# Weight granules of an attention and two-MLP kernel: one sum of squares and one pair of scale operations for two granules instead of one

## The chip, the cores and the metric

The kernel runs on one core of a Trainium2 chip. The metric is the device time of one execution in microseconds (us). Five engines work side by side, each through its own list of instructions in order: TensorE (PE in the profile, PEld for its weight loads), VectorE (DVE), ScalarE (ACT), GpSimd (POOL) and SyncE (SP), which here issues the transfers.

## The reference

```python
scores = scale * np.matmul(q, k.transpose(0, 1, 3, 2))      # 4 batches, 8 heads, 576 positions, 64 per head
masks = [mask_local if h < H // 2 else mask_strided ...]     # a window of 32, or every 32nd position
attn = softmax(np.where(masks, scores, -1e9))
x = np.matmul(attn, v)                                       # -> 2304 tokens of 512
h = x @ w_in                                                 # 512 -> 2048
g = (a0 + a1*h + a2*h*h + a3*h*h*h) / (1 + |b0|*|h| + |b1|*h*h + 1e-6)
x = g @ w_out                                                # 2048 -> 512
h = x @ w_in2                                                # 512 -> 1024
solu = h * softmax(h)
out = (layer_norm(solu) * g_ln) @ w_out2                     # 1024 -> 512
```

The weights arrive as 64-bit floats. All products of the two MLPs have float32 accuracy, made from 16-bit operands.

## The kernel before, in words

A product with float32 accuracy is made of three 16-bit matmuls: high part times high part, high times low, low times high. So each weight has two 16-bit tiles, for `w_in` `wi_h` and `wi_l`, for `w_out` `wo_h` and `wo_l`, and before the split each block of a weight is multiplied by a power of two that brings it into the range of a 16-bit float.

The two large weights come in eight granules each. A granule of `w_in` ("wi") is 256 of its 2048 columns, which is what one group of the first product needs; a granule of `w_out` ("wo") is 64 of its 512 output columns. So a block of 128 output columns of the second product needs two wo granules, and all four blocks need all eight. For each granule:

- SP loads the 64-bit words (`w_load`) into a staging place; most of these are tiles that are free at that time, such as `wo_h`, `ysb` or `ws`.
- `w_conv` makes 32-bit floats of them with three bit operations on DVE (L151, L152, L153) into a tile `T`, into a piece of `gtb` or `ysb`, or into a place of staging that is done with.
- ACT squares them and sums along each partition (L160). The sum goes to `ss`, a small tile of which there are two. PE adds it over the partitions with a matrix of ones (L84). DVE makes from the exponent of the sum the power of two `pat` (L163) and its inverse `scl` (L164).
- `w_split` writes the high part on ACT (L181), and on DVE the low part (L182), which needs the high part.

The first batch of the attention (12 units: scores on PE, maximum and sums on DVE, exponentials on ACT, a product on POOL, transposes and the product with v on PE) runs from the start to about 66 us, while `w_in` is loaded and converted. After it the first product starts. It is made of groups of 256 columns of `h` and blocks of 256 tokens, 72 groups: 24 matmuls in `mm_h` (L532 to L534) into `ps_h`, of which there are two, then the rational function on ACT, POOL and DVE (ACT L540 to L571, POOL L549 and L553, DVE L557 to L583), which gives `ps_h` free again at L583, then the high and low parts of the result (ACT L593, POOL L597), then 24 matmuls of the second product in `mm_y` (L609 to L611). The later batches of the attention, the conversion of the second MLP's weights and the second MLP itself are interleaved with these groups.

The order of the instructions on every engine isn't written out by hand. A scheduler plays the program through with a model of its own and places instructions by when they would be ready and by a priority that `prio` sets; each engine then runs its list in that order. An instruction that waits therefore holds up everything behind it on its engine.

The lines of the code around the change, in the main part: wi granules are converted and split one after the other with priorities 10000 + 300 g, wo granules in `wo_work` with `p_step(g)`, two in each of the first four steps:

```python
    for g in range(8):
        prio(10000 + 300 * g)
        w_conv("wi", g)
        w_split("wi", g)
```

Of the kernel before, what the change touches and what calls it, by code (L numbers as in the profile page):

```python
# [8 lines left out]
F32 = mybir.dt.float32  # L9
# [3 lines left out]
AF = mybir.ActivationFunctionType  # L13
# [27 lines left out]
def kernel(ctx: ExitStack, tc: tile.TileContext, qk, v, w_in, w_out, ab, w_in2, w_out2, gln, out):  # L41
    nc = tc.nc
    PE, ACT, DVE, POOL, SP = nc.tensor, nc.scalar, nc.vector, nc.gpsimd, nc.sync

    const = ctx.enter_context(tc.tile_pool(name="const", bufs=1))
# [15 lines left out]
    gtb = wts.tile([128, NGT, 2, 2, TB], F16, name="gtb")  # L61
    ysb = wts.tile([128, NYS, 2, KD, TB], F16, name="ysb")
# [10 lines left out]
    def psum(tag, shape=(128, 512), bufs=1):  # L73
        return ps.tile(list(shape), F32, tag=tag, name=f"ps_{tag}", bufs=bufs)

    def t1(name, n=1, bufs=2):
        return tiny.tile([128, n], F32, tag=name, name=name, bufs=bufs)

    def ew(name, bufs, shape=(128, 512), dt=F32):
        return big.tile(list(shape), dt, tag=name, name=name, bufs=bufs)  # L80

    def sum_over_partitions(x):
        t = psum("a", bufs=2)[:, 0:x.shape[1]]
        PE.matmul(t, lhsT=ones_f, rhs=x, start=True, stop=True)  # L84
        return t
# [9 lines left out]
    NGRAN = {"wi": 8, "wo": 8}  # L95
    pat = {k: const.tile([128, n], F32, name=f"pat_{k}") for k, n in NGRAN.items()}
    scl = {k: const.tile([128, n], F32, name=f"scl_{k}") for k, n in NGRAN.items()}
# [21 lines left out]
    def w_load(name, g):  # L119
        if name == "wi":  # L120
            src = w_in.bitcast(I32)[:, g * 512:(g + 1) * 512].rearrange("(k p) f -> p k f", p=128)
        elif name == "wo":
            src = w_out.bitcast(I32)[:, g * 128:(g + 1) * 128].rearrange("(k p) f -> p k f", p=128)
        elif name == "wi2":
            src = w_in2.bitcast(I32)[g * 128:(g + 1) * 128, :]
        else:
            src = w_out2.bitcast(I32)[g * 256:(g + 1) * 256, :].rearrange("(k p) f -> p k f", p=128)
        t = w_slot(name, g)
        if name == "wi2":
            SP.dma_start(out=t, in_=src)  # L130
        else:
            SP.dma_start(out=t.rearrange("p (k f) -> p k f", f=src.shape[2]), in_=src)
        stg[name, g] = t

    def w_conv(name, g):
        t = stg.pop((name, g))
        if name in ss2:
            if g == 2:
                w2t[name] = ew("ws", 1, (128, 2048), I32).bitcast(F32)
            T = ew("T", 2, (128, 1024), F32) if g < 2 else w2t[name][:, 1024 * (g - 2):1024 * (g - 1)]  # L140
        elif name == "wo" and g % 5 > 1:
            T = ysb[:, 2].rearrange("p h d t -> p (h d t)") if g == 4 else gtb[:, 2 * (g % 5) - 4:2 * (g % 5) - 2].rearrange("p b c h t -> p (b c h t)")
            T = T.bitcast(F32)
        else:
            T = spare.pop() if spare else ew("T", 2, (128, 1024), F32)
        if name == "wi" and g < 7:
            spare.append(t[:, 0:1024].bitcast(F32))
        t = t.rearrange("p (f two) -> p f two", two=2)
        lo, hi = t[:, :, 0], t[:, :, 1]
        Ti = T.bitcast(I32)  # L150
        DVE.tensor_scalar(Ti, hi, 3, 0x3FFFFFFF, op0=ALU.logical_shift_left, op1=ALU.bitwise_and)  # L151
        DVE.scalar_tensor_tensor(Ti, lo, 29, Ti, op0=ALU.logical_shift_right, op1=ALU.bitwise_or)  # L152
        DVE.scalar_tensor_tensor(Ti, hi, -0x40000000, Ti, op0=ALU.bitwise_and, op1=ALU.bitwise_or)  # L153
        tt[name, g] = T
        if name in ss2:
            ACT.activation(ew("ot", 1).bitcast(F16), T, AF.Square, accum_out=ss2[name][:, g:g + 1])
            return
        ss = t1("ss")
        src, junk, _ = w_parts(name, g, T)
        ACT.activation(junk, src, AF.Square, accum_out=ss)  # L160
        sg = sum_over_partitions(ss)
        p, s = pat[name][:, g:g + 1], scl[name][:, g:g + 1]
        DVE.tensor_scalar(p.bitcast(I32), sg.bitcast(I32), 1, EXPM, op0=ALU.logical_shift_right, op1=ALU.bitwise_and)  # L163
        DVE.tensor_scalar(s.bitcast(I32), p.bitcast(I32), -1.0, float(EXPM - (51 << 23)), op0=ALU.mult, op1=ALU.add)  # L164

# [3 lines left out]
    def w_parts(name, g, T):  # L169
        if name == "wi":  # L170
            sl = slice(g * 256, g * 256 + 256)
            return T.rearrange("p (k f) -> p k f", k=KD), wi_h[:, :, sl], wi_l[:, :, sl]
        sl = slice(g * 64, g * 64 + 64)
        return T.rearrange("p (k f) -> p k f", k=KF), wo_h[:, :, sl], wo_l[:, :, sl]

    def w_split(name, g):
        s = scl[name][:, g:g + 1]
        if g == NGRAN[name] - 1:
            DVE.tensor_scalar(inv[name], pat[name], 2.0 ** 50, None, op0=ALU.mult)
        src, h_, l_ = w_parts(name, g, tt.pop((name, g)))  # L180
        ACT.activation(h_, src, AF.Copy, scale=s)  # L181
        DVE.scalar_tensor_tensor(l_, src, s, h_, op0=ALU.mult, op1=ALU.subtract)  # L182
# [30 lines left out]
    def w_pmax(name):  # L213
        m = t1("pm")
        DVE.tensor_reduce(m, pat[name], axis=AX.X, op=ALU.max)
        DVE.tensor_scalar(pmax[name], m, 2.0 ** 65, None, op0=ALU.mult)
# [514 lines left out]
    def prio(p):  # L731
        tc.cur_priority = p
# [8 lines left out]
    def p_step(n):  # L741
        return P0 + int(n * P_STEP)
# [53 lines left out]
    for g in range(8):  # L796
        prio(10000 + 300 * g)
        w_conv("wi", g)
        w_split("wi", g)
    prio(900)  # L800
    w_pmax("wi")
    g_scale(0)
# [114 lines left out]
    def wo_work(g):  # L917
        w_conv("wo", g)
        if g + 4 < 8:
            w_load("wo", g + 4)  # L920
        w_split("wo", g)
        if g == 7:
            w_pmax("wo")
            for j in range(2):
                sl = slice(64 * j, 64 * j + 64)
                POOL.tensor_copy(cwo[sl, :], inv["wo"][sl, j::2])

    def w2_work(n):
        for name, n0 in (("wi2", 14), ("wo2", 21)):
            m = n - n0  # L930
            if m == 0:
                w_load(name, 0)
                w_load(name, 1)
            if m in (1, 2):
                for g in (2 * m - 2, 2 * m - 1):
                    w_conv(name, g)
                    if g < 2:
                        w_load(name, g + 2)
                if m == 2:
                    w2_scale(name)  # L940
            if m in (3, 4):
                w2_split(name, 2 * m - 6)
                w2_split(name, 2 * m - 5)

    for n in range(M2S + 4 * (NT2 + 2)):
        if 0 <= n < 4:
            for g in (2 * n, 2 * n + 1):
                prio(p_step(g))
                wo_work(g)
        prio(p_step(n + 2))  # L950
        w2_work(n)
        prio(p_step(n))
        if n >= M2S and (n - M2S) % 8 == 0 and (n - M2S) // 8 < NB:
            y_scale2((n - M2S) // 8)
        step(n)
# [56 lines left out]
```

## Time and profile before

| | |
|---|---|
| time, three runs | 804.7, 797.74, 805.2 us (median 804.7) |
| the profiled execution's own time | 799.58 us |
| its span, first to last instruction | 797.2 us |
| busy share of the span | PE 89%, DVE 72%, ACT 61%, POOL 41% |
| mean granted TensorE clock | 0.928 of full speed |
| chain of work that ended last, by engine | PE 58%, DVE 15%, DMA 5%, ACT 5%, issue 4%, POOL 3% |

A busy share is a mean over stages that have different limits, so the stages are read apart: the windows view gives each engine's busy time in a stretch with the granted clock, the timeline lists one engine's instructions with their start, duration and the idle time ahead of them with what ended it.

### The profile page before, as it was taken

The page shows a single profiled execution, that of the slowest core. Times are in us where ns is not written, and L with a number is a line of the kernel's source. Part 1 is how long each engine was busy: PE and PEld are TensorE (multiplying, and loading weights), DVE is VectorE, ACT ScalarE, POOL GpSimd, SP SyncE. Part 2 cuts the span into 40 slices and gives each one's busy share as a digit, 9 for nine tenths or more (in the row PEclk, how much of TensorE's full clock was granted, in tenths as well). Part 3 has the DMA queues.
Part 4 walks back from the last instruction along what each step waited for, and adds up shares of the span by engine and source line. Part 5 has one row for each costly group of instructions (what it writes and reads, how often), then busy time and mean ns, then how long its engine had stood idle before and what let it go on. Part 6 is the DMA issues. An engine that isn't in the chain of part 4 may idle for free.

```text
span 797.2 us, 14480 instructions
## 1 busy us (share of the span) xinstructions
PE 707.4 (89%) x5422; PEld 539.7 (68%) x5422; DVE 573.0 (72%) x1210; ACT 483.4 (61%) x1143; POOL 327.2 (41%) x312
## 2 busy tenths in 40 slices
PE   4785146988886999899999999999999999999997
PEld 4664135877674788587878777777777777766443
DVE  5788899779869886688987666757657666644562
ACT  3656475756756687866777666646546556543442
POOL 2530303545557567745545443344343434330000
PEclk8565656999999999899999999999999999999999
DMA  9985511053130431113031101011012020111134
GB/s 271 350 207 139 159 53 33 1 171 92 54 118 1 138 86 40 33 28 92 2 72 33 41 1 41 1 41 40 1 41 35 7 40 8 34 41 40 39 80 106
DMA packets 68101, 55.98 MB, mean 70 GB/s; under 512 B 39616, under 2 KB 56000, under 8 KB 67520
## 3 DMA queue, kind: packets, MB, share of 16 engines
q1 hardware_dynamic: 68032, 55.07, 25.8%
q8 instruction: 42, 0.69, 0.4%
q14 instruction: 27, 0.22, 0.1%
HBM read 40.90 MB, written 4.72 MB: 57 GB/s over the span
## 4 chain that ended last, share of the span: by engine, by line
PE 58%; DVE 15%; DMA 5%; ACT 5%; issue 4%; POOL 3%; SPq 0%; DVEq 0%; ACTq 0%; POOLq 0%
PE ps_h L532 6%; PE ps_h L534 6%; PE ps_h L533 6%; PE ps_y L611 6%; PE ps_y L610 6%; PE ps_y L609 6%; PE ps_h L642 3%; PE ps_h L643 3%; PE ps_h L644 3%; PE ps_a L722 3%; PE ps_a L721 3%; PE ps_a L720 3%; PE ps_a L289 2%; DMA wi_h<-in_w_in_dram 1%; PE ps_a L380 1%
## 5 line engine op out<-in xcount | busy, mean ns | idle before, releaser
L532 PE MATMUL ps_h<-xs,wi_h 128*128 128x256 f16 x576 | 160.4, 279 | 12.1 <-DVE p L583 9.2
L533 PE MATMUL ps_h<-xs,wi_h 128*128 128x256 f16 x576 | 160.2, 278 | 0.0
L534 PE MATMUL ps_h<-xs,wi_l 128*128 128x256 f16 x576 | 159.9, 278 | 0.2 <-DVE wi_l L182 0.2
L597 POOL TENSOR_TENSOR gtb<-p,gtb 128x512 f16<-128x512 f32 x56 | 67.1, 1199 | 134.8 <-ACT gtb L593 134.6
L611 PE MATMUL ps_y<-gtb,wo_l 128*128 128x256 f16 x448 | 122.1, 273 | 0.0
L610 PE MATMUL ps_y<-gtb,wo_h 128*128 128x256 f16 x448 | 122.1, 273 | 0.0
L609 PE MATMUL ps_y<-gtb,wo_h 128*128 128x256 f16 x448 | 122.1, 273 | 0.0
L549 POOL TENSOR_SCALAR q<-A,aba 128x512 f32<-128x512 f32 x72 | 62.6, 869 | 108.6 <-ACT A L540 108.5
L553 POOL TENSOR_TENSOR q<-q,A 128x512 f32<-128x512 f32 x72 | 96.6, 1342 | 5.7
L557 DVE TENSOR_TENSOR p<-p,ps_h 128x512 f32<-128x512 f32 x72 | 49.2, 683 | 57.6 <-ACT p L543 53.2
L566 ACT ACTIVATE L<-q 128x512 f32<-128x512 f32 x72 | 45.3, 630 | 70.0 <-POOL q L553 69.8
L575 DVE SCALAR_TENSOR_TENSOR q<-q,ps_h 128x512 f32<-128x512 f32 x72 | 49.2, 683 | 36.5 <-ACT ps_h L571 35.4
L533 PEld LDWEIGHTS <-wi_h 128*128 128x128 f16 x576 | 57.6, 100 | 16.6 <-issue 8.4
L532 PEld LDWEIGHTS <-wi_h 128*128 128x128 f16 x576 | 57.7, 100 | 13.3 <-ACT wi_h L181 3.0
L540 ACT ACTIVATE A<-ps_h,ih 128x512 f32<-128x512 f32 x72 | 49.2, 684 | 28.0 <-PE ps_h L534 26.2
L593 ACT ACTIVATE gtb<-p 128x512 f16<-128x512 f32 x56 | 35.3, 631 | 50.6 <-DVE p L583 50.5
L610 PEld LDWEIGHTS <-wo_h 128*128 128x128 f16 x576 | 56.4, 98 | 10.7
L609 PEld LDWEIGHTS <-wo_h 128*128 128x128 f16 x576 | 56.6, 98 | 10.1
L534 PEld LDWEIGHTS <-wi_l 128*128 128x128 f16 x576 | 57.5, 100 | 8.2 <-DVE wi_l L182 0.3
L340 POOL TENSOR_TENSOR e<-e,arc 96x508 f32<-96x508 f32 (+3 forms) x36 | 37.4, 1039 | 62.2 <-DVE arc L339 48.6
L611 PEld LDWEIGHTS <-wo_l 128*128 128x128 f16 x576 | 56.4, 98 | 8.1 <-issue 1.1
L331 ACT ACTIVATE e<-ps_a,amx 96x127 f32<-96x127 f32 (+2 forms) x132 | 45.8, 356 | 16.8 <-DVE amx L315 12.7
(336 smaller groups left out, 1825.0 us busy)
## 6 DMA issues: line engine op xcount, KB each, us to landing
qkb<-in_qk_dram SPq DMA_DIRECT2D x28, 304.0 KB, 4.5
out_dram<-ot SPq DMA_DIRECT2D x18, 256.0 KB, 2.5
wo_l<-in_w_out_dram SPq DMA_DIRECT2D x4, 1024.0 KB, 5.4
wo_h<-in_w_out_dram SPq DMA_DIRECT2D x4, 1024.0 KB, 5.3
vl<-in_v_dram SPq DMA_DIRECT2D x4, 768.0 KB, 5.3
wi_h<-in_w_in_dram SPq DMA_DIRECT2D x3, 1024.0 KB, 7.0
wi_l<-in_w_in_dram SPq DMA_DIRECT2D x3, 1024.0 KB, 5.2
wo_h<-in_w_in_dram SPq DMA_DIRECT2D x3, 1024.0 KB, 16.5
```

The costliest lines, as they stand in the source:

```text
L532: PE.matmul(o, lhsT=wi_h[:, k, f:f + 128], rhs=xs[i][:, 0, k, :], start=(k == 0), stop=False)
L533: PE.matmul(o, lhsT=wi_h[:, k, f:f + 128], rhs=xs[i][:, 1, k, :], start=False, stop=False)
L534: PE.matmul(o, lhsT=wi_l[:, k, f:f + 128], rhs=xs[i][:, 0, k, :], start=False, stop=(k == KD - 1))
L540: ACT.activation(A, t, AF.Abs, scale=gsc[i]["ih"][:, g:g + 1])
L549: POOL.tensor_scalar(w["q"], w["A"], aba[:, 5:6], aba[:, 4:5], op0=ALU.mult, op1=ALU.add)
L553: POOL.tensor_tensor(w["q"], w["q"], w["A"], op=ALU.mult)
L557: DVE.tensor_tensor(w["p"], w["p"], hp[i, g], op=ALU.mult)
L575: DVE.scalar_tensor_tensor(w["q"], w["q"], EPS_D, w["r"], op0=ALU.add, op1=ALU.mult)
L597: POOL.tensor_tensor(t[:, :, 1, :], gw.pop((i, g))["p"].rearrange("p (c t) -> p c t", t=TB), t[:, :, 0, :], op=ALU.subtract)
L609: PE.matmul(o, lhsT=wo_h[:, f, w], rhs=gg[:, c, 0, :], start=(f == 0 and d % 2 == 0), stop=False, skip_group_check=True)
L610: PE.matmul(o, lhsT=wo_h[:, f, w], rhs=gg[:, c, 1, :], start=False, stop=False, skip_group_check=True)
L611: PE.matmul(o, lhsT=wo_l[:, f, w], rhs=gg[:, c, 0, :], start=False, stop=(f == KF - 1), skip_group_check=True)
```

## The change

Pairs of granules take the step from the sum of squares to the scale together. The sums of squares go to a tile of eight columns for each weight, `ssq`, instead of the two small tiles `ss`. A new function `w_scales` adds two columns over the partitions with one L84 and makes two columns of `pat` and `scl` with one L163 and one L164. For wi, all eight conversions stand ahead in the program; the scale steps and splits follow pair by pair. For wo, the scale step and both splits stand after the second conversion of a pair. The tile into which a wo granule is converted is chosen with period 4 instead of 5: granules 2, 3, 6 and 7 go to `gtb`, granules 0, 1, 4 and 5 to `T`; before, 2, 3 and 7 went to `gtb`, 4 to `ysb`, and 0, 1, 5 and 6 to `T`.

```diff
-        elif name == "wo" and g % 5 > 1:
-            T = ysb[:, 2].rearrange("p h d t -> p (h d t)") if g == 4 else gtb[:, 2 * (g % 5) - 4:2 * (g % 5) - 2].rearrange("p b c h t -> p (b c h t)")
-            T = T.bitcast(F32)
+        elif name == "wo" and g % 4 > 1:
+            j = 2 * (g % 4) - 4
+            T = gtb[:, j:j + 2].rearrange("p b c h t -> p (b c h t)").bitcast(F32)
...
-        ss = t1("ss")
         src, junk, _ = w_parts(name, g, T)
-        ACT.activation(junk, src, AF.Square, accum_out=ss)
-        sg = sum_over_partitions(ss)
-        p, s = pat[name][:, g:g + 1], scl[name][:, g:g + 1]
+        ACT.activation(junk, src, AF.Square, accum_out=ssq[name][:, g:g + 1])
+
+    ssq = {k: const.tile([128, n], F32, name=f"ssq_{k}") for k, n in NGRAN.items()}
+
+    def w_scales(name, g0, n):
+        sg = sum_over_partitions(ssq[name][:, g0:g0 + n])
+        p, s = pat[name][:, g0:g0 + n], scl[name][:, g0:g0 + n]
         DVE.tensor_scalar(p.bitcast(I32), sg.bitcast(I32), 1, EXPM, op0=ALU.logical_shift_right, op1=ALU.bitwise_and)
         DVE.tensor_scalar(s.bitcast(I32), p.bitcast(I32), -1.0, float(EXPM - (51 << 23)), op0=ALU.mult, op1=ALU.add)
...
     for g in range(8):
         prio(10000 + 300 * g)
         w_conv("wi", g)
-        w_split("wi", g)
+    for g0 in range(0, 8, 2):
+        prio(10000 + 300 * g0)
+        w_scales("wi", g0, 2)
+        for g in range(g0, g0 + 2):
+            prio(10000 + 300 * g)
+            w_split("wi", g)
...
         w_conv("wo", g)
         if g + 4 < 8:
             w_load("wo", g + 4)
-        w_split("wo", g)
+        if g % 2 == 2 - 1:
+            w_scales("wo", g + 1 - 2, 2)
+            for j in range(g + 1 - 2, g + 1):
+                prio(p_step(j))
+                w_split("wo", j)
```

The scheduler places the instructions of the whole program anew. In the changed kernel the line numbers are higher: L160, L163, L164, L181 and L182 are L159, L166, L167, L184 and L185 there, and lines of the later functions are three higher. The three places below are the ones that matter for what follows.

ACT at the end of the first attention batch. `q<-ps_a`, `xs<-ps_a` and `tail<-ps_a` belong to the last attention units; the L160 rows (L159 in the change) are the squares of wi granules, named by the place that their 32-bit values lie in. Before:

```order
L358 ACTIVATE q<-ps_a 108x2x108
L411 ACTIVATE xs<-ps_a,xsc_184 128x8x6 x2
L408 ACTIVATE tail<-ps_a 128x2x6
L160 ACTIVATE wi_h,ss<-wi_l 128x4x256
L160 ACTIVATE wi_h,ss<-wo_h 128x4x256
L160 ACTIVATE wi_h,ss<-ysb 128x4x256
L181 ACTIVATE wi_h<-T,scl_wi 128x4x256
L160 ACTIVATE wi_h,ss<-wo_h 128x4x256 x2
L181 ACTIVATE wi_h<-wi_h,scl_wi 128x4x256
```

And in the change, from the square of granule 6 on:

```order
L159 ACTIVATE wi_h,ssq_wi<-wo_h 128x4x256
L361 ACTIVATE q<-ps_a 108x2x108
L334 ACTIVATE p,smb_104<-ps_y,amx 108x108 x2
...
L361 ACTIVATE q<-ps_a 108x4x108
L159 ACTIVATE wi_h,ssq_wi<-wo_l 128x4x256
L414 ACTIVATE xs<-ps_a,xsc_186 128x8x12 x2
...
L184 ACTIVATE wi_h<-T,scl_wi 128x4x256
L184 ACTIVATE wi_h<-wi_h,scl_wi 128x4x256
```

Six of the eight squares of wi move from behind the attention units to places among them, and the eight splits follow one another.

DVE where the wo granules are scaled. L557 to L583 (L560 to L586 in the change) belong to the rational function of groups 0 and 1. Before:

```order
L163 TENSOR_SCALAR pat_wo<-ps_a 128x1
L182 SCALAR_TENSOR_TENSOR wo_l<-T,scl_wo,wo_h 128x16x64
L426 TENSOR_SCALAR rg<-pg_743 128x1
L164 TENSOR_SCALAR scl_wo<-pat_wo 128x1
L163 TENSOR_SCALAR pat_wo<-ps_a 128x1
L151 TENSOR_SCALAR T<-ysb 128x1024
...
L182 SCALAR_TENSOR_TENSOR wo_l<-gtb,scl_wo,wo_h 128x16x64
L557 TENSOR_TENSOR p<-p,ps_h 128x512
```

And in the change:

```order
L166 TENSOR_SCALAR pat_wo<-ps_a 128x2
L560 TENSOR_TENSOR p<-p,ps_h 128x512
L167 TENSOR_SCALAR scl_wo<-pat_wo 128x2
L166 TENSOR_SCALAR pat_wo<-ps_a 128x2
L560 TENSOR_TENSOR p<-p,ps_h 128x512
L564 SCALAR_TENSOR_TENSOR p<-p,ac_728,ps_h 128x512
L92 TENSOR_REDUCE vmax_830<-ps_a 128x1
L167 TENSOR_SCALAR scl_wo<-pat_wo 128x2
L564 SCALAR_TENSOR_TENSOR p<-p,ac_728,ps_h 128x512
L185 SCALAR_TENSOR_TENSOR wo_l<-T,scl_wo,wo_h 128x16x64
```

The first steps of groups 0 and 1 now stand ahead of the first wo splits; before, they stood behind four of them. In the whole list four L583 of `ps_h` groups stand ahead of the last wo split, before it was two.

PE at the last sums over the partitions for wo. Before, the last two L84 stand ahead of any matmul of groups 2 and 3:

```order
L350 MATMUL ps_a<-ident,e 127x96 x4
L380 MATMUL ps_a<-pts,vl 64x96 x4
L84 MATMUL ps_a<-ss,ones_f 128x1 x2
```

In the change, groups 2 and 3 and the first six matmuls of the second product stand ahead of the third pair's L84, and the fourth pair's stands here:

```order
L353 MATMUL ps_a<-ident,e 127x96 x4
L383 MATMUL ps_a<-pts,vl 64x96 x4
L612 LDWEIGHTS wo_h
L612 MATMUL ps_y<-wi_h,wo_h 128x256
L613 LDWEIGHTS wo_h
L613 MATMUL ps_y<-wi_h,wo_h 128x256
L84 MATMUL ps_a<-ssq_wo,ones_f 128x2
```

The two matmuls into `ps_y` ahead of it use the third pair's split. On SP, the load of `vs` (the second batch) moves behind the loads of wo granules 6 and 7; before, it stood ahead of both.

## Rows read from the trace of the kernel before

**Rows 1.** The page: busy times of the engines, granted clock in 40 slices.
```profile
PE 707.4 (89%) x5422; PEld 539.7 (68%) x5422; DVE 573.0 (72%) x1210; ACT 483.4 (61%) x1143; POOL 327.2 (41%) x312
...
PEclk8565656999999999899999999999999999999999
```

**Rows 2.** Windows: stretch, its length, busy time (instructions) by engine, clock, DMA share, GB/s.
```profile
66.00:132.00 66.00, 25.20 (x136) 21.61 (x137) 60.62 (x141) 41.51 (x75) 10.89 (x7) 0.55 0.39 106
132.00:260.00 128.00, 110.46 (x993) 93.44 (x991) 103.77 (x220) 84.50 (x221) 73.93 (x68) 0.99 0.23 74
260.00:340.00 80.00, 75.00 (x653) 62.41 (x653) 60.15 (x121) 61.99 (x157) 55.18 (x51) 0.94 0.24 73
340.00:700.00 360.00, 360.00 (x2878) 275.63 (x2878) 252.98 (x520) 225.88 (x494) 159.25 (x149) 1.00 0.14 31
```

**Rows 3.** Timeline of ACT: start, duration (us), line, operation, count, [idle before <-what ended it].
```profile
67.03 1.06 ACT L160 ACTIVATE wi_h<-wi_l 128x1024 f16<-128x1024 f32 x1
...
69.94 1.06 ACT L160 ACTIVATE wi_h<-wo_h 128x1024 f16<-128x1024 f32 x1 [1.76 <-PE ps_a L84]
...
71.00 1.04 ACT L160 ACTIVATE wi_h<-ysb 128x1024 f16<-128x1024 f32 x1
...
80.39 1.04 ACT L160 ACTIVATE wi_h<-wo_l 128x1024 f16<-128x1024 f32 x1
...
85.56 1.15 ACT L181 ACTIVATE wi_h<-wo_l,scl_wi 128x1024 f16<-128x1024 f32 x1 [1.80 <-DVE inv_wi L179]
```

**Rows 4.** Timeline of DVE, 46 to 137 us.
```profile
46.73 0.74 DVE L315 TENSOR_REDUCE amx<-ps_y 126x2 f32<-126x252 f32 x2 [0.41 <-PE ps_y L289]
...
52.07 0.38 DVE L315 TENSOR_REDUCE amx<-ps_h 108x2 f32<-108x216 f32 x1 [0.97 <-PE ps_h L289]
...
77.40 1.28 DVE L182 SCALAR_TENSOR_TENSOR wi_l<-wi_h,scl_wi 128x1024 f16<-128x1024 f32 x1 [2.09 <-ACT wi_h L181]
...
85.33 0.14 DVE L164 TENSOR_SCALAR scl_wi<-pat_wi 128x1 int32<-128x1 int32 x1
85.39 0.16 DVE L179 TENSOR_SCALAR inv_wi<-pat_wi 128x8 f32<-128x8 f32 x1
...
87.30 0.69 DVE L151 TENSOR_SCALAR T<-wo_h 128x1024 int32<-128x1024 int32 x1 [1.69 <-DMA wo_h<-in_w_out_dram]
...
91.09 1.21 DVE L153 SCALAR_TENSOR_TENSOR T<-wo_h,T 128x1024 int32<-128x1024 int32 x1
...
96.37 0.16 DVE L163 TENSOR_SCALAR pat_wo<-ps_a 128x1 int32<-128x1 int32 x1 [0.87 <-PE ps_a L84]
96.45 2.05 DVE L153 SCALAR_TENSOR_TENSOR T<-ysb,T 128x1024 int32<-128x1024 int32 x1
...
104.36 0.69 DVE L151 TENSOR_SCALAR T<-ysb 128x1024 int32<-128x1024 int32 x1 [0.66 <-DMA ysb<-in_w_out_dram]
...
136.23 1.27 DVE L182 SCALAR_TENSOR_TENSOR wo_l<-gtb,scl_wo,wo_h 128x1024 f16<-128x1024 f32 x1
```

**Rows 5.** DMA issues, 62 to 80 us: count, KB each, us to landing.
```profile
wo_l<-in_w_out_dram SPq DMA_DIRECT2D x1, 1024.0 KB, 5.8
vs<-in_v_dram SPq DMA_DIRECT2D x1, 640.0 KB, 4.2
```

**Rows 6.** Timeline of POOL, 88 to 98 us.
```profile
90.04 3.38 POOL L553 TENSOR_TENSOR q<-q,A 128x512 f32<-128x512 f32 x1
...
96.16 1.26 POOL L553 TENSOR_TENSOR q<-q,A 128x512 f32<-128x512 f32 x1
```

**Rows 7.** Timeline of PE: two neighbouring matmuls at the lower clock; the longest later idle time.
```profile
75.12 0.42 PE L533 MATMUL ps_h<-xs,wi_h 128*128 128x256 f16 x1
75.33 0.42 PE L534 MATMUL ps_h<-xs,wi_l 128*128 128x256 f16 x1
...
259.65 0.96 PE L350 MATMUL ps_a<-ident,e 96*127 96x96 f32 x4 [5.05 <-POOL e L340]
```

**Rows 8.** The page: matmuls that start a group, idle time before them and what ended most.
```profile
L532 PE MATMUL ps_h<-xs,wi_h 128*128 128x256 f16 x576 | 160.4, 279 | 12.1 <-DVE p L583 9.2
```

## The prediction

> **What bounds the kernel now.** I read the page first. TensorE is busy for 89% of the span, and its granted clock is low only in the first seven of forty slices, about 140 us [rows 1]. So the question is when TensorE becomes full and what holds it until then. The windows answer it: from 340 to 700 us PE is busy for 360 of 360 us at full clock, and nothing on another engine can shorten that stretch. From 66 to 132 us it is busy for 25.2 of 66 us at a clock of 0.55, while DVE is busy for 60.6 of 66 us. Between 132 and 340 us, PE is idle for 17.5 + 5.0 = 22.5 us [rows 2]. The 66 to 132 us stretch is where the two large weights are converted, scaled and split, so what the change does there is read from DVE's queue: whatever delays the last wo split on DVE (from 136.23 us, [rows 4]) delays the second product, and whatever DVE gets done by then beside the weights is a lead for PE.
>
> Next I looked at why DVE and ACT wait there. The third square of wi starts on ACT only at 67.03 us, and the next one waits for an L84 [rows 3]: there are two `ss` tiles, so a third square has to wait until the first L84 has read its tile, and PE's queue has that L84 behind the last attention unit. The last square of wi runs at 80.39 us and the last high part at 85.56 us. DVE pays for this with 2.09 us at 77.40 us, where it waits for a high part [rows 4].
>
> **The change part by part.** The sum is made against the profiled execution, 799.6 us with a span of 797.2 us. The three runs have a median of 804.7 us, which is 0.6% above it; the mean of all four executions is 801.8 us.
>
> *Squares and splits of wi.* With eight columns of `ssq` no square waits for an L84, and the change's order puts six squares among the attention units, with the eight splits one after another. DVE's 2.09 us go. What is late next is DVE itself: a low part takes it 1.28 us [rows 4], a high part takes ACT 1.15 us [rows 3]. I take 2.1, between 0 and 2.1.
>
> The squares aren't free at their new place. ACT takes its list in order, so each square holds up the attention units behind it until its granule is converted. Start to start a square takes 71.00 - 69.94 = 1.06 us [rows 3], so six cost between nothing and 6.4 us. ACT has room, and DVE gains there: the conversions move up in its list, into four idle times between 46.73 and 52.07 us (0.41, 0.68, 0.37 and 0.97 us, the first and the last in [rows 4]), 2.4 us together. I take 2.4 - 1.0 = 1.4 for both, since the squares stand where ACT waits for PE anyway; the ends are +2.4 and -4.0.
>
> *Fewer scale operations.* Eight L163 and eight L164 go. On DVE such an operation takes 0.14 us but the next starts after 0.06 us (85.33 to 85.39, [rows 4]). So the sixteen are worth 16 x 0.06 = 1.0 us at least and 16 x 0.14 = 2.2 us at most; I take 1.0, because DVE's queue moves on by starts. The eight L84 that go run while PE is idle: nothing.
>
> *Transfers.* DVE waits 1.69 us for the load of wo granule 0 at 87.30 us and 0.66 us for granule 5 at 104.36 us [rows 4]. In the change's list the conversion of granule 0 stands behind the last split of wi instead of ahead of it, and that of granule 5 behind the first four wo splits, so both loads have cover: 2.3, between 0 and 2.3. On the other side `vs` is loaded behind 1 MB more on SP. A load of 1 MB lands after 5.8 us, `vs` after 4.2 us [rows 5], and the maximum over `vs` stands between the third and the fourth wi split, ahead of what gives the staging of granule 0 free. I take -0.5, between 0 and -5.8.
>
> *The pairs of wo.* The first L163 of wo now needs two conversions, two squares and their L84. Before, it waited 0.87 us for one [rows 4]. The second square adds up to 1.06 us; between the conversion and the L163 stand the eight or so small operations of the rational function's constants. I take -0.3, between +0.9 and -1.1.
>
> *PE's queue.* The third pair's L84 is now behind 48 matmuls of groups 2 and 3 and six of the second product. Group 3 may start only when DVE has finished L583 of group 1. Behind this L84 waits DVE's L163, and behind that everything on DVE. At the low clock a group takes 24 x 0.21 = 5.0 us (75.12 to 75.33, [rows 7]). So this costs between nothing, when the squares of granules 4 and 5 are later than group 3, and 5.0 us; I take -3.0, as DVE has L583 of group 1 directly ahead of two conversions of 1.2 us that fill only 2.4 us.
>
> *POOL beside DVE.* Two more groups pass through L549 and L553 while DVE converts. L553 takes 3.38 us at 90.04 us and 1.26 us at 96.16 us; L153 on DVE takes 1.21 us at 91.09 us and 2.05 us at 96.45 us, beside that L553 [rows 4, 6]. Two groups cost DVE between nothing and 2 x 0.84 = 1.7 us; POOL's own 2 x 2.1 us are hidden, since the results are needed later. I take -1.0. The Trainium skill, "SBUF — State Buffer", § Who interferes with whom, says that a DVE instruction with two SBUF inputs and a GpSimd instruction that reads SBUF exclude one another for the whole instruction. The stretched rows agree. By that rule each added L553 could hold DVE for its whole 1.26 us, and this term would be -2.5, the sum 1.5 us smaller.
>
> *What the lead is worth later.* At 259.65 us PE is idle for 5.05 us ahead of four transposes that wait for POOL [rows 7]. In the change's PE list the 24 matmuls of a group stand ahead of these transposes. At full clock they are some 24 x 0.11 = 2.6 us (half of the low clock's 0.21). I take +1.3, between 0 and 2.6.
>
> Sum: 2.1 + 1.4 + 1.0 + 2.3 - 0.5 - 0.3 - 3.0 - 1.0 + 1.3 = 3.3 us saved. Against the profiled execution this is 796.3 us; against the mean of the four executions 798.5 us. As the runs shown lie on both sides I give **798 us**. With all terms at their good ends the change saves 2.1 + 2.4 + 2.2 + 2.3 + 0.9 + 2.6 = 12.5 us (789 us); at their bad ends it saves 1.0 and loses 4.0 + 5.8 + 1.1 + 5.0 + 1.7 = 17.6 us, net 16.6 (818 us), and these need not come together.
>
> **The rivals.** One per cent is 8 us here, about what this kernel's runs can tell from no change.
>
> *The lead removes later waits too (faster).* By the last wo split the change's DVE list holds four L583, before it was two. PE's idle time at the start of a group is 12.1 us, 9.2 of it waiting for L583 [rows 8]. If rational functions stay two groups ahead, these waits go: 3.3 + 9.2 = 12.5 us saved, 789 us. For it speaks that PE's idle time there has this one main cause; against it that the scheduler uses the lead to place the second MLP's conversions differently, so that by group 15 the lists stand alike again.
>
> *PE's queue decides (slower).* The fourth pair's L84 stands behind scores, transposes, the product with v and two matmuls that need the third pair's split, and these wait for ACT, which has the evacuation of the transposes between the two splits. So the two last pairs go one after the other: DVE makes the third pair's scale, ACT splits, PE passes, and only then comes the fourth pair's scale. Each step holds a whole group at the low clock, 5.0 us, and two squares and splits, 2 x (1.06 + 1.15) = 4.4 us, so up to 9.4 us for a pair instead of the 3.0 that I took. If both pairs pay it all, DVE has its other work to fill perhaps half: 18.8 / 2 - 3.0 = 6.4 us more than in my sum, 3.1 us lost net, 805 us. It decides when the fourth pair's L163 begins later than about 6 us after the third pair's. Against it: DVE has three groups' worth of the rational function in between.
>
> *It is hidden anyway (no change).* The first split may not come earlier, as its scale now stands behind all conversions of wi and the last attention unit, and the wo loads follow the wi splits. Then the waits that go come back as waits for transfers and pairs: 802 us.
>
> **How the numbers follow.** Chances: the sum as forecast 0.48, the lead kept 0.22, PE's queue 0.17, no change 0.13. Faster by over 1%: nearly all of the lead's 0.22 and a seventh of the forecast's, 0.28. Slower by over 1%: a half of the queue's, with the bad ends of the squares and of `vs`, and a little of the others, 0.13. Within 1%: 0.59. The range from 787 to 809 us takes in the lead's 789, the queue's 805 with 4 us for the unknown ends, and leaves out one in ten on each side. The forecast's own range is 794 to 803.
>
> **What would show it.** In the changed kernel's profile the squares of wi should stand before about 70 us and the eight splits on ACT without a gap. DVE should have no wait over 0.5 us for a high part and none for wo granule 0. The wait of PE for L583 at group 3, followed by a DVE wait for the third pair's L84, would show the term of 3 us; the end of the last wo split should lie between 137 and 144 us with four L583 ahead of it. If that split ends after 147 us, or the first split of wi begins after 74 us, or PE has more than 22.5 us of idle time between 132 and 340 us, the forecast is wrong.

## The result, and the profile after

The changed kernel takes 795.0 us (median of 20 runs, 789.9 to 799.9), the kernel before 803.7 us on the same chip. The ratio is 0.9906, with a 95% interval from 0.9887 to 0.9924. With its order written out again (below) it came to 0.9875 (0.9854 to 0.9895) on another chip. The change saves about 1%, 7.5 to 10 us. The forecast was 798 us, a saving of 3.3 us. Every ratio in this document is to the kernel before on the same chip. Medians leave out single executions in a slower state.

The page of the changed kernel (lines from 160 on are three higher than before: L535 was L532, L586 was L583, L166 was L163):
```profile
PE 705.6 (89%) x5406; PEld 534.3 (68%) x5406; DVE 570.7 (72%) x1194; ACT 481.6 (61%) x1143; POOL 329.0 (42%) x312
...
PEclk8665557999999999999999999999999999999999
...
L535 PE MATMUL ps_h<-xs,wi_h 128*128 128x256 f16 x576 | 161.1, 280 | 25.9 <-DVE p L586 25.8
```
Against [rows 8], the wait for L586 has grown from 9.2 to 25.8 us, and still the kernel is faster. A wait total by itself is no price: the waits have moved into a stretch in which PE was idle before, too. From 66 to 132 us PE is idle for 39.1 us, before for 40.8 us [rows 2].

Windows of the changed kernel, first as in [rows 2], then cut where the differences lie:
```profile
66.00:132.00 66.00, 26.93 (x174) 20.88 (x175) 63.59 (x133) 40.14 (x75) 23.14 (x12) 0.63 0.36 97
132.00:260.00 128.00, 118.00 (x1042) 98.75 (x1042) 104.84 (x221) 86.91 (x229) 75.45 (x65) 0.97 0.28 89
260.00:340.00 80.00, 71.71 (x616) 59.03 (x616) 58.79 (x128) 60.18 (x159) 50.64 (x51) 0.96 0.17 48
340.00:700.00 360.00, 359.87 (x2869) 274.68 (x2868) 252.60 (x515) 224.78 (x485) 155.74 (x149) 1.00 0.15 31
...
70.00:170.00 100.00, 62.13 (x493) 51.87 (x494) 88.21 (x191) 64.66 (x139) 43.29 (x34) 0.75 0.30 83
170.00:240.00 70.00, 65.14 (x598) 55.74 (x597) 56.75 (x106) 48.73 (x124) 41.70 (x36) 1.00 0.31 100
240.00:340.00 100.00, 87.13 (x728) 69.74 (x727) 78.57 (x178) 71.53 (x192) 62.20 (x59) 0.95 0.20 59
```
The same cut of the kernel before:
```profile
70.00:170.00 100.00, 61.09 (x476) 53.07 (x477) 84.84 (x199) 64.98 (x137) 32.35 (x29) 0.72 0.32 87
170.00:240.00 70.00, 59.66 (x552) 51.31 (x550) 57.09 (x106) 46.45 (x124) 37.58 (x35) 1.00 0.30 99
240.00:340.00 100.00, 88.23 (x748) 71.75 (x746) 78.63 (x169) 74.86 (x188) 70.07 (x61) 0.95 0.20 59
```
The span fell by 797.2 - 790.5 = 6.7 us. PE's busy time fell by 1.85 us (707.43 to 705.58 in the sums of the windows). The other 4.85 us are idle time (length less busy time): 1.04 us less from 70 to 170 us (38.91 to 37.87), **5.48 us less from 170 to 240 us** (10.34 to 4.86), 1.10 us more from 240 to 340 us, 0.57 us more in all the rest. So in this profile most of the gain is not in the stage of the weights, where the change was made, but 30 to 100 us behind it.

A second profile of the same order (the changed kernel with its order written out, below; its span is 788.6 us) divides the gain otherwise:
```profile
70.00:170.00 100.00, 65.32 (x513) 53.42 (x513) 89.79 (x188) 64.01 (x136) 44.74 (x34) 0.76 0.29 80
170.00:240.00 70.00, 63.50 (x575) 54.00 (x573) 57.37 (x112) 49.30 (x128) 41.28 (x36) 1.00 0.31 100
240.00:340.00 100.00, 87.97 (x744) 71.20 (x744) 78.55 (x173) 72.58 (x192) 61.81 (x60) 0.95 0.19 59
```
There PE is idle for 34.68 us from 70 to 170 us, 4.2 us less than before, and for 6.50 us from 170 to 240 us, 3.8 us less. The gain from 170 to 240 us is in both profiles, 3.8 and 5.5 us. That of the weights' stage is 4.2 us in one and 1.0 us in the other, because executions differ in when this stage begins (last section). A cut that moves with the kernel is the start of the last wo split. From there to the end of the span the kernel before takes 797.2 - 136.2 = 661.0 us, the changed kernel 790.5 - 138.7 = 651.8 us and, in the second profile, 788.6 - 137.0 = 651.6 us. So the gain lies behind this cut: up to it the changed kernel is 2.5 and 0.8 us later than the kernel before, though with more done.

What PE waited for from 170 to 240 us (us in total, times, longest), before and then in the changed kernel:
```profile
PE ps_h L532 <- DVE p L583: 6.2, 5, 2.0
```
```profile
PE ps_h L535 <- DVE p L586: 2.0, 1, 2.0
```
In the stage of the weights, the timeline of ACT in the changed kernel answers to [rows 3]:
```profile
62.78 0.59 ACT L361 ACTIVATE q<-ps_a 126x504 f32<-126x504 f32 x1 [3.83 <-PE ps_a L353]
...
66.53 1.06 ACT L159 ACTIVATE wi_h<-wo_l 128x1024 f16<-128x1024 f32 x1 [0.26 <-DVE wo_l L153]
...
71.16 1.15 ACT L184 ACTIVATE wi_h<-T,scl_wi 128x1024 f16<-128x1024 f32 x1 [0.58 <-DVE scl_wi L167]
...
78.45 1.13 ACT L184 ACTIVATE wi_h<-wo_l,scl_wi 128x1024 f16<-128x1024 f32 x1
```
The last square stands at 66.53 us instead of 80.39 us, and the eight high parts follow one another from 71.16 to 79.58 us. The timeline of DVE answers to [rows 4]:
```profile
83.62 1.23 DVE L485 TENSOR_TENSOR ih<-ih,ih 128x8 f32<-128x8 f32 x1
...
86.42 0.68 DVE L151 TENSOR_SCALAR T<-wo_h 128x1024 int32<-128x1024 int32 x1
...
89.15 1.16 DVE L151 TENSOR_SCALAR T<-ysb 128x1024 int32<-128x1024 int32 x1 [0.32 <-DMA ysb<-in_w_out_dram]
...
95.88 0.16 DVE L166 TENSOR_SCALAR pat_wo<-ps_a 128x2 int32<-128x2 int32 x1 [0.68 <-PE ps_a L84]
...
124.08 0.15 DVE L166 TENSOR_SCALAR pat_wo<-ps_a 128x2 int32<-128x2 int32 x1
...
133.10 0.14 DVE L166 TENSOR_SCALAR pat_wo<-ps_a 128x2 int32<-128x2 int32 x1
...
138.71 1.36 DVE L185 SCALAR_TENSOR_TENSOR wo_l<-gtb,scl_wo,wo_h 128x1024 f16<-128x1024 f32 x1
```
No wait for a high part is left, none for the load of wo granule 0, and none for the L84 of the third and fourth pair. The last wo split ends at 140.07 us, 2.6 us later than before, but with four L586 ahead of it (112.62, 119.40, 131.18 and 137.93 us) instead of two.

POOL, as in [rows 6], and PE, as in [rows 7]:
```profile
82.60 2.22 POOL L556 TENSOR_TENSOR q<-q,A 128x512 f32<-128x512 f32 x1
```
```profile
113.41 0.39 PE L535 MATMUL ps_h<-xs,wi_h 128*128 128x256 f16 x1 [14.03 <-DVE p L586]
...
269.46 0.27 PE L535 MATMUL ps_h<-xs,wi_h 128*128 128x256 f16 x1 [3.21 <-DVE p L586]
```
The 14.03 us at 113.41 us are the bulk of the 25.8: group 2 now stands ahead of the transposes in PE's list and waits there. The 5.05 us at 259.65 us are gone, but 3.21 us at 269.46 us have come in the neighbourhood. Of [rows 5], `vs` now takes 6.7 us to land instead of 4.2:
```profile
vs<-in_v_dram SPq DMA_DIRECT2D x1, 640.0 KB, 6.7
```

### The profile page after: what moved, and what is told of

It is laid out like the page before. It is cut to its first block, busy times and chain, and to the rows that moved or that the text cites. A ratio compares the mean times of both kernels' runs of the same rounds, so it can differ in the third digit from the quotient of the medians.

```text
span 790.5 us, 14385 instructions
## 1 busy us (share of the span) xinstructions
PE 705.6 (89%) x5406; PEld 534.3 (68%) x5406; DVE 570.7 (72%) x1194; ACT 481.6 (61%) x1143; POOL 329.0 (42%) x312
## 4 chain that ended last, share of the span: by engine, by line
PE 70%; DVE 14%; DMA 5%; ACT 5%; issue 4%; POOL 2%; SPq 1%; ACTq 0%; DVEq 0%; POOLq 0%
PE ps_h L535 7%; PE ps_y L613 7%; PE ps_y L614 7%; PE ps_y L612 7%; PE ps_h L537 7%; PE ps_h L536 7%; PE ps_h L647 3%; PE ps_h L646 3%; PE ps_h L645 3%; PE ps_a L292 3%; PE ps_a L725 3%; PE ps_a L723 3%; PE ps_a L724 3%; PE ps_a L383 3%; DMA wi_h<-in_w_in_dram 2%
## 5 line engine op out<-in xcount | busy, mean ns | idle before, releaser
L535 PE MATMUL ps_h<-xs,wi_h 128*128 128x256 f16 x576 | 161.1, 280 | 25.9 <-DVE p L586 25.8
L600 POOL TENSOR_TENSOR gtb<-p,gtb 128x512 f16<-128x512 f32 x56 | 66.0, 1178 | 119.5 <-ACT gtb L596 119.5
L552 POOL TENSOR_SCALAR q<-A,aba 128x512 f32<-128x512 f32 x72 | 62.7, 870 | 105.3 <-ACT A L543 105.1
L556 POOL TENSOR_TENSOR q<-q,A 128x512 f32<-128x512 f32 x72 | 99.1, 1377 | 5.3
L560 DVE TENSOR_TENSOR p<-p,ps_h 128x512 f32<-128x512 f32 x72 | 49.2, 683 | 48.3 <-ACT p L546 46.3
L535 PEld LDWEIGHTS <-wi_h 128*128 128x128 f16 x576 | 58.0, 101 | 31.0 <-DVE p L586 21.9
L343 POOL TENSOR_TENSOR e<-e,arc 96x508 f32<-96x508 f32 (+3 forms) x36 | 38.9, 1081 | 62.6 <-DVE arc L342 41.6
```

What stands on the lines that cost most here:

```text
L535: PE.matmul(o, lhsT=wi_h[:, k, f:f + 128], rhs=xs[i][:, 0, k, :], start=(k == 0), stop=False)
L552: POOL.tensor_scalar(w["q"], w["A"], aba[:, 5:6], aba[:, 4:5], op0=ALU.mult, op1=ALU.add)
L556: POOL.tensor_tensor(w["q"], w["q"], w["A"], op=ALU.mult)
L560: DVE.tensor_tensor(w["p"], w["p"], hp[i, g], op=ALU.mult)
L600: POOL.tensor_tensor(t[:, :, 1, :], gw.pop((i, g))["p"].rearrange("p (c t) -> p c t", t=TB), t[:, :, 0, :], op=ALU.subtract)
```

## The experiments

Theory A: the two `ss` tiles were the cost. Theory B: sharing the sums and scales saves. Theory C: the stage of the weights gives some 3 us, and the rest comes from how the planner (the scheduler) lays out the work behind it. The first four kernels let the planner order them anew.

**Columns alone.** The kernel before with eight columns in place of the tile:
```diff
-        ss = t1("ss")
-        ACT.activation(junk, src, AF.Square, accum_out=ss)
+        ACT.activation(junk, src, AF.Square, accum_out=ssq[name][:, g:g + 1])
...
```


> The order of the code, the single L84 and the single pair of scale operations per granule as before; only the two ss tiles are replaced by eight columns of ssq. Theory A (the two ss tiles were the cost: a third square waited for an L84 behind the attention units): most of the 8.7 us between the medians comes from here, 796 to 798 us, squares of wi before 70 us and no wait of DVE over 0.5 us for a high part. Theory B (sharing is what saves: sixteen tiny operations and eight L84 fewer, and two splits behind one scale): 802 to 804 us. Theory C (the stage of the weights gives some 3 us, the rest depends on how the planner lays out the work after 140 us): squares early as in A, last wo split 2 to 4 us earlier or with more L583 ahead of it, but a time anywhere between 792 and 803 us, decided by PE's idle time between 132 and 340 us.

Measured: 814.5 us, ratio 1.0167 (1.0131 to 1.0204). An edit meant only to take a wait away makes the kernel 1.7% slower: A falls, and the time is also outside C's 792 to 803 us. From 260 to 280 us PE is busy for 11.9 of 20 us, at a clock of 0.65:
```profile
260.00:280.00 20.00, 11.90 (x65) 8.73 (x63) 17.98 (x33) 9.65 (x25) 6.53 (x5) 0.65 0.50 162
```

**The changed kernel with single scales**, ordered anew:
```diff
-        w_scales("wi", g0, 2)
+        w_scales("wi", g0, 1)
+        w_scales("wi", g0 + 1, 1)
...
-            w_scales("wo", g + 1 - 2, 2)
+            w_scales("wo", g - 1, 1)
+            w_scales("wo", g, 1)
```


> The changed kernel with its pairs of splits and its staging of wo, but each granule with an L84 and a pair of scale operations of its own (16 scale operations and 8 L84 more). Theory A: sharing is worth at most the 1.0 to 2.2 us of the sixteen operations on DVE, 796 to 797 us. Theory B: the gain goes, 801 to 804 us. Theory C: the stage of the weights ends at most 2 us later than in the changed kernel, the time lies anywhere between 792 and 803 us.

Measured: 802.5 us, ratio 1.0029 (1.0000 to 1.0058): what B asks for. It is inside C's range of time, but not as C had it: the last wo split starts at 144.34 us, 5.6 us later than in the changed kernel, where C allowed 2 us.

**One half of the change each**: pairs for wi with wo as before (its staging too, which is not shown), and the reverse.
```diff
-        if g % 2 == 2 - 1:
-            w_scales("wo", g + 1 - 2, 2)
-            ...
+        w_scales("wo", g, 1)
+        w_split("wo", g)
```


> The part of the change for wi alone (columns, pairs); wo with its staging of before and one scale per granule, though with columns too. Theory A: about all of the gain, 795 to 798 us, since the tiles held up wi. Theory B: half of the gain, 799 to 800 us. Theory C: first high part of wi at 71 us as in the changed kernel, the time anywhere between 792 and 803 us.

> The part of the change for wo alone (pairs of splits behind one scale, staging with period 4); wi with one scale per granule in the order of before, but with columns. Theory A: as the columns alone, 795 to 798 us. Theory B: half of the gain, 799 to 800 us. Theory C: the time lies anywhere between 792 and 803 us; four L583 ahead of the last wo split if the pairs of wo are what lets the groups pass, two if the columns of wi are not enough for it.

Measured: 808.0 us (1.0095, 1.0060 to 1.0130) and 811.1 us (1.0123, 1.0074 to 1.0171). Each half is slower than the kernel before; by B each should have half of the gain. The sizes do not add up. Ahead of the last wo split stand two L586 with the wi half and four with the wo half, so the pairs of wo are what lets four groups pass; the time is 811 us all the same. C's range of 792 to 803 us was missed by three of the four kernels. What is left of C is that each edit gives another order of the whole program.

To part the order from the edit, the next kernels have it written out. A list gives the place of every instruction on its engine, and each is tied to its forerunner by an edge that sets the order alone, without a semaphore:
```diff
+        for a, b in zip(order, order[1:]):
+            tc.add_manual_dep(queue[b], queue[a].name, info, reason="order")
```
An order is cut behind the last wo split: "early" is what stands ahead of the cut, "late" what stands behind it. Line numbers are one higher in these kernels.

**Old and new, exchanged at the cut.**

> The changed kernel, with the order of every engine written out: up to the last wo split the order of the changed kernel, behind it the order of the kernel before. Theory E (the gain arises in the stage of the weights, and what comes later only carries it): 795 to 797 us, as the changed kernel. Theory L (the planner's later order makes the difference): the 2.6 us of TensorE's lead at 132 us stay, the later 4 to 6 us go, 799 to 802 us, and the idle time ahead of the transposes that wait for POOL near 260 us is back.

> The kernel before (two ss tiles, one scale per granule), with its own order up to the last wo split and the order of the changed kernel behind it. Theory E: 802 to 805 us, as the kernel before. Theory L: 797 to 800 us, as only the 2.6 us of the first stage are missing from the changed kernel's time.

| ratio to before | late old | late new |
|---|---|---|
| early old | 1 | 1.0112 (1.0066 to 1.0158) |
| early new | 1.0010 (0.9975 to 1.0046) | 0.9906 (0.9887 to 0.9924) |

New then old takes 801.9 us, old then new 809.3 us. The first is what L expected; the second is above both theories. Windows and waits of PE (170 to 240 us) in new then old:
```profile
130.00:170.00 40.00, 34.36 (x299) 28.78 (x301) 27.69 (x68) 25.74 (x73) 18.11 (x19) 0.87 0.21 58
170.00:240.00 70.00, 59.47 (x539) 50.59 (x534) 57.22 (x105) 44.62 (x123) 35.43 (x33) 0.98 0.30 99
...
PE ps_h L536 <- DVE p L587: 6.2, 5, 2.2
```
and in old then new:
```profile
130.00:170.00 40.00, 33.76 (x278) 28.98 (x279) 29.02 (x72) 24.07 (x58) 21.70 (x22) 0.88 0.07 17
170.00:240.00 70.00, 63.60 (x589) 54.58 (x587) 54.76 (x105) 45.83 (x128) 35.00 (x32) 0.99 0.36 114
...
PE ps_h L533 <- DVE p L584: 1.8, 1, 1.8
```
The five waits of 6.2 us belong to the old late order, with the new lead as without it, and so do the 5.1 us ahead of the transposes that wait for POOL: both came back in new then old. The new late order has one wait of 1.8 to 2.0 us. So the saving from 170 to 240 us is a property of the late order. Counted from the start of the last wo split,
```profile
142.27 1.27 DVE L186 SCALAR_TENSOR_TENSOR wo_l<-gtb,scl_wo,wo_h 128x1024 f16<-128x1024 f32 x1
```
```profile
137.88 1.27 DVE L183 SCALAR_TENSOR_TENSOR wo_l<-gtb,scl_wo,wo_h 128x1024 f16<-128x1024 f32 x1
```
new then old takes 802.5 - 142.3 = 660.2 us to its end, nearly the 661.0 us of the kernel before, although four L587 stand ahead of the cut; old then new takes 807.6 - 137.9 = 669.7 us. Against the kernel before, neither the lead nor the new late order is worth anything by itself; with both, the changed kernel takes 651.8 us.

From 130 to 170 us PE is idle for 5.6 and 6.2 us in the mixtures, against 0.4 us before and 1.5 us in the changed kernel. In new then old the largest part is a wait that the changed kernel has as well, just ahead of this window, because its stage of the weights began 3.6 us earlier; new then old and the changed kernel:
```profile
132.87 0.91 PE L384 MATMUL ps_a<-pts,vl 127*64 127x96 f32 x8 [4.28 <-ACT pts L362]
```
```profile
129.31 0.91 PE L383 MATMUL ps_a<-pts,vl 127*64 127x96 f32 x8 [4.29 <-ACT pts L361]
```
In old then new it is a wait behind the cut: there the new late order asks for a rational function that the old early order has not made ready.
```profile
146.53 0.39 PE L533 MATMUL ps_h<-xs,wi_h 128*128 128x256 f16 x1 [5.29 <-DVE p L584]
```

**The columns' early order, the new late order.**

> The kernel with only the eight columns (814.5 us in its own order), with its own order up to the last wo split and the order of the changed kernel behind it. Theory E (its early order has cost the 13.6 us): still 808 to 815 us. Theory L (its later order costs it, with the low clock between 260 and 340 us): 795 to 800 us, and no granted clock under 0.8 in 260 to 280 us.

Measured: 803.1 us, ratio 1.0036 (1.0005 to 1.0067), below E's range and above L's. Of the 1.67% that the columns cost in their own order, 1.3 points were the late order; from 260 to 280 us PE is back at 16.6 us and a clock of 0.93:
```profile
260.00:280.00 20.00, 16.57 (x143) 13.74 (x142) 17.30 (x46) 12.47 (x36) 9.76 (x8) 0.93 0.29 85
```
**The price of sharing alone**, in the order of the changed kernel.

> Each granule with its own L84 and its own two scale operations, but every other instruction in the order of the changed kernel, the added ones directly ahead of those of the pair. This is the price of sharing alone: my term says 1.0 us (16 x 0.06 us on DVE), at most 2.2 us, so 796 to 797.5 us by theory L. By the theory that sharing is the cause, 801 to 804 us, as the kernel with single scales had in its own order.

> The changed kernel itself, with its own order written out: every instruction, wait and engine order is that of the changed kernel. It is the measure for the next ones. Both theories: a ratio to the kernel before of 0.988 to 0.993.

> The order of the changed kernel; wi with an L84 and two scale operations for each granule (four more of each), wo in pairs. Theory R (each scale more is one more trip from L84 to L163 through the two PSUM tiles, 0.42 us of DVE in the row of eight): 4 x 0.42 = 1.7 us later at the splits of wi and 1 to 4 us at the end, depending on what TensorE gets by then; 797 to 799 us where the changed kernel has 795. Theory of the small price (0.06 us per operation on DVE): 8 x 0.06 = 0.5 us, not to be told from the changed kernel. If it is as slow as the kernel with all scales single, wo's share of that loss is nothing.

| scales of wi, of wo | time | ratio to before |
|---|---|---|
| 4 and 4 (the change) | 791.4 us | 0.9875 (0.9854 to 0.9895) |
| 8 and 4 | 794.8 us | 0.9924 (0.9903 to 0.9945) |
| 8 and 8 | 805.1 us | 1.0058 (1.0028 to 1.0088), other chip |

In the order of the changed kernel sharing is worth far more than my 1.0 us: 0.5 points (3.4 us) for wi, as theory R expected, and 1.3 points more for wo, by kernels on two chips. Without sharing the new order gains nothing: 805.1 us is just above the 801 to 804 us of the theory that sharing is the cause. The size of wo's part stays open: counted from the first L167 to the end of the span, eight scales of wi take 793.0 - 67.7 = 725.3 us where four take 719.8 us, and all scales single take 799.0 - 71.7 = 727.3 us, only 2.0 us more; that profiled run, 800.8 us, is the second fastest of its twelve. The first and last L167 of wi and the last wo split, with four scales of wi and then with eight:
```profile
68.77 0.16 DVE L167 TENSOR_SCALAR pat_wi<-ps_a 128x2 int32<-128x2 int32 x1 [0.83 <-PE ps_a L85]
...
70.47 0.16 DVE L167 TENSOR_SCALAR pat_wi<-ps_a 128x2 int32<-128x2 int32 x1
...
136.98 1.36 DVE L186 SCALAR_TENSOR_TENSOR wo_l<-gtb,scl_wo,wo_h 128x1024 f16<-128x1024 f32 x1
```
```profile
67.67 0.16 DVE L167 TENSOR_SCALAR pat_wi<-ps_a 128x1 int32<-128x1 int32 x1 [0.82 <-PE ps_a L85]
68.50 0.16 DVE L167 TENSOR_SCALAR pat_wi<-ps_a 128x1 int32<-128x1 int32 x1 [0.68 <-PE ps_a L85]
...
71.47 0.16 DVE L167 TENSOR_SCALAR pat_wi<-ps_a 128x1 int32<-128x1 int32 x1 [0.27 <-PE ps_a L85]
...
138.38 1.36 DVE L186 SCALAR_TENSOR_TENSOR wo_l<-gtb,scl_wo,wo_h 128x1024 f16<-128x1024 f32 x1
```
Four scales take 1.70 us from first to last, eight 3.80 us: 2.1 us for four scales, because DVE waits at most of them for the next sum (L85). The PSUM buffer `a` has two tiles, so the third L85 cannot start before the first L167 has read. From the first L167 to the start of the last wo split it is 68.21 us with four and 70.71 us with eight. With wo single too, PE itself waits at such an L85:
```profile
138.45 0.59 PE L85 MATMUL ps_a<-ssq_wo,ones_f 128*128 128x1 f32 x2 [2.28 <-DVE pat_wo L167]
```
**One scale for all of wi**, in the order of the changed kernel:
```diff
-    for g0 in range(0, 8, 2):
+    for g0 in range(0, 8, 8):
...
-        w_scales("wi", g0, 2)
+        w_scales("wi", g0, 8)
-        for g in range(g0, g0 + 2):
+        for g in range(g0, g0 + 8):
```


> The order of the changed kernel; all eight granules of wi by one L84 and two scale operations (three fewer of each), wo in pairs. Theory R: 3 x 0.42 = 1.3 us fewer on DVE ahead of the first low part, but the high parts on ACT follow one another from the first scale on, so DVE waits for the first one instead: 0 to 1.5 us gained. Theory of the small price: 6 x 0.06 = 0.4 us, no difference.

Measured: 794.2 us, ratio 0.9914 (0.9891 to 0.9936), 2.8 us slower than the pairs. The first low part waits for its high part and comes 1.81 us after the first L167 (75.44 - 73.63), with pairs 1.82 us: sharing beyond pairs has nothing left to save there. In the profiled runs nothing behind the first scale is slower: from the first L167 to the end it takes 791.6 - 73.6 = 718.0 us, with pairs 788.6 - 68.8 = 719.8 us. But its run began the scales 4.9 us later than the one with pairs, with every engine in the same order until then. Why, and whether the other five runs did the same, stays open.

**A candidate to beat both.**

> The kernel with pairs for wi alone (808.0 us in its own order), with its own order up to the last wo split, behind it the order of the changed kernel. By its trace TensorE lost 46.7 us (idle time and low clock) from 70 to 170 us, against 48.0 in the changed kernel. Theory L (the planner's later order decides, if it fits what is ready at 140 us): 793 to 797 us, a candidate to beat both. Theory F (an order planned for another start does not fit; so it was with both exchanges of old and new): TensorE idle for 5 to 6 us or more from 130 to 170 us, 800 to 806 us.

Measured: 802.6 us, ratio 1.0020 (0.9997 to 1.0044); PE is idle for 7.0 us from 130 to 170 us. F holds, L does not: 4.62 us of it are a wait for L587 at 141.90 us, just behind the cut. Still the new late order is better for this kernel than its own (1.0095). No version beat the changed kernel.

## Why the prediction was right, and where its sum was not

The range held and the class (within 1%) is the one that I had given 0.59, but in part by luck. The saving was 8.7 us instead of 3.3; 795.0 us lies between my 798 us and the 789 us of the rival of the lead; the interval of the ratio reaches past 1%, and the second measurement, 0.9875 with 791.4 us, is outside the class and the forecast's own range (794 to 803). The signs in the weights' stage came as described: the early squares, the splits without a gap, the last wo split at 140 us behind four L586. Most of the terms were off in size, and what the kernel gained most came from the place to which I had given 1.3 us.

- **Squares and splits of wi** (+2.1): right. The wait for a high part is gone.
- **Softmax stage** (+1.4): not shown. ACT waits 3.83 us at 62.78 us, and the last evacuation there starts at 70.02 us, before at 66.52 us; the first split came 0.87 us earlier all the same (71.16 against 72.03). But executions of one order differ here by up to 6.5 us (last section), so one profile each decides neither.
- **Scale operations** (+1.0): the mis-sized term. I counted starts on DVE (0.06 us) and missed the trip from DVE to PE and back through two PSUM tiles. In the order of the changed kernel, where the scales of wi stand in a row, it costs 2.1 us for four scales, and the whole kernel became 3.4 us slower. The short durations hide it, since the price is the wait ahead of each. But the kernel before did not pay this price: its L163 of wi stand between conversions and splits, and DVE waits at none of the eight, while the changed kernel waits at its first two, here before and then changed.
```profile
73.26 0.21 DVE L163 TENSOR_SCALAR pat_wi<-ps_a 128x1 int32<-128x1 int32 x2
...
79.80 0.15 DVE L163 TENSOR_SCALAR pat_wi<-ps_a 128x1 int32<-128x1 int32 x1
```
```profile
70.52 0.16 DVE L166 TENSOR_SCALAR pat_wi<-ps_a 128x2 int32<-128x2 int32 x1 [0.82 <-PE ps_a L84]
...
71.36 0.16 DVE L166 TENSOR_SCALAR pat_wi<-ps_a 128x2 int32<-128x2 int32 x1 [0.24 <-PE ps_a L84]
```
So sharing is what makes the row of scales affordable. What it saves against the order of before, no run shows.
- **Transfers** (+2.3): 1.69 + 0.66 us became 0.32 us, 2.0 us saved. `vs` (-0.5) took 2.5 us longer to land; DVE shows no wait for it.
- **The pairs of wo** (-0.3): the first L166 waits 0.68 us, before 0.87: +0.2.
- **PE's queue** (-3.0): nothing. PE did wait 1.94 us for L586 at 120.19 us, but DVE found the third pair's sum ready at 124.08 us. The rival built on it (805 us) fell with this: the fourth pair's L166 came 9.0 us after the third's, and yet DVE waited for neither, because it had work between. The delay was the wrong test; the wait is the right one.
- **POOL beside DVE** (-1.0): from 66 to 140 us nine instructions of DVE took over 0.1 us longer than most of their form, some 5 us together; before there were six, some 3 us together: about -2. L485, 128x8, takes 1.23 us at 83.62 us, beside the L556 from 82.60 to 84.82 us; both end together. The Trainium skill, "SBUF — State Buffer", § Who interferes with whom, has such a DVE instruction wait for the whole of POOL's, and this row agrees. Its sum of -2.5 came nearer than my -1.0, in part by luck: it was made of two L556, and five of the nine stand beside no L556 but beside L552, L600 or L343.
- **The lead later** (+1.3): 5.5 us from 170 to 240 us, 3.8 us in the second profile. The wait of 5.05 us that the term was made of went, but from 240 to 340 us PE is idle for 1.1 us more. The rival "the lead removes later waits" named the right wait (L583) and had 9.2 us for it. But its reason fails: with the new lead and the old late order all 6.2 us of these waits are there. The late order removes them, and it is planned together with the early one. What I called against this rival, that the planner lays things out differently, was in fact what made the gain.

In sum the stretch from 70 to 170 us gave 1.0 us of PE's idle time in one profile and 4.2 us in the other, where I had 2.0 (the sum without the later 1.3), and the later order the rest. That the planner found such an order was no part of the change's own logic: four other edits of the same lines, each sensible, gave between 1.0029 and 1.0167.

## What to carry to other kernels

Where a scheduler lays out the whole program, time an edit also with the order held fixed, and its parts alone: here the sharing and the new order were both worth several us, each only with the other, and neither half of the edit was faster than nothing. Where small operations that cross engines stand in a row, price them by the round trip through the buffers between them, not by their duration. Where the start of a kernel varies, count from an instruction and not from the start of the span: fixed windows took the same wait of 4.3 us in once and left it out once. An order found for one start need not fit another: the new late order cost 1.1% behind the old start, but gained 1.3 points behind the columns and 0.75 points behind the pairs of wi.

## What the runs showed of the hardware

The first stage varies by itself. Six kernels had the same order on every engine up to the first scale of wi, and in their profiled runs it came at 67.67, 68.77, 70.52, 71.68, 73.63 and 74.14 us. The conversion of the first granule in `ws` begins on DVE at 51.64, 52.76, 54.49, 55.64, 57.59 and 58.10 us, always 16.0 us ahead of it, so the whole spread of 6.5 us is there by then. In the four later ones DVE waits 0.48 to 1.39 us for the load of `ws` at that place, in the two early ones not at all; the loads have a part in it, but what delays them was not tried. From the first high part of wi to the end, the changed kernel's two profiled runs agree within 0.1 us (719.3 and 719.2), though their spans differ by 1.9 us.
